# Attention and routed experts on one core: loads for eight heads at once, and traded halves in one block of keys

## The chip, the cores and the metric

One NeuronCore of a Trainium2 chip runs the whole program. The metric is the device time of one execution in microseconds. A kernel's time is the median of its runs; one more execution is taken by the profiler, and its times are the ones quoted from views of the profile.

## The reference

Attention over 8 batches with 8 heads, 576 positions and head size 64, where a position sees all keys of its own block of 64 and of the blocks before; then a mixture of 8 experts, in which each position is sent through one expert, chosen by its own logits or taken over from the position before it.

```python
scores = scale * np.matmul(q, k.transpose(0, 1, 3, 2))
mask = block_i >= block_j                      # pos // 64
scores = np.where(mask, scores, -1000000000.0)
attn = softmax(scores)
x = np.matmul(attn, v)                         # heads side by side: 512 columns
...
logits, local_gate = x @ w_gate, sigmoid(x @ w_local)
e = argmax(logits[b, s]) if s == 0 or local_gate[b, s] < 0.5 else prev_e
h = np.maximum(x[b, s] @ w1[e], 0.0)
out[b, s] = softmax(logits[b, s])[e] * (h @ w2[e])
```

The inputs and the result are float32; the expert weights are rounded to bf16 on the chip.

## The kernel before

**Tiles and loops.** The attention runs over 32 pairs of heads (pair `i` is batch `i // 4`, heads `2 * (i % 4)` and the next), in one loop in whose step `i` several stages lie side by side: the loads of `k` and `q` of pair `i + 2`, the value products of pair `i - 1`, the scores and exponentials of pair `i`, and the transposes of `k` and `q` of pair `i + 1`. Behind the attention come the experts, tile by tile of 128 positions. Routing steps on VectorE (DVE) are spread over the pairs.

**Scores and values.** Scores are held with keys on partitions and queries on columns. The 576 keys make chunks 0 to 3 of 128 keys and chunk 4 of 64. Within a chunk, `scores` computes each half of 64 keys apart, in float32 for two heads, so that four products of 64 x 64 stand in the four quarters of TensorE's array. The later half of a chunk is not seen by the chunk's first 64 queries. There chunk 0 holds the scores of chunk 4 instead, and the other chunks get a large negative number from a bf16 product (`minus` times `ones_b`, line 975), of which the exponential is zero. `values` then multiplies: for chunks 0 to 3 the list `VALUES` says from which query on and how many columns (two heads in the two column halves of the array, all 128 keys deep), and at the end, behind whatever is put `between`, come chunk 4 and the first 64 queries of chunk 0, 64 keys deep each, in the upper and the lower row half (line 1007). `add_chunks` sums the exponentials on VectorE for the denominators.

**Loads.** All loads of `q`, `k` and `v` are issued by SyncE (SP) in the program's order. `load_qk` brings the first 512 rows of `k` and `q` of a pair (256 KB each) into a staging place in the last two experts' part of `w2_bf`, and the 64 rows of the tail of each (32 KB) into a small tile `qkl`. GpSimd (POOL) rearranges the staged rows (`arrange`, line 880) before TensorE turns them (`transposes`, line 692, tiles `kq` and, for the tails, `o`). `load_v` brings `v` of a pair: two loads of 128 KB into a tile `v4`, with two buffers, and the 64 rows of the tail into `vl`. A load into a buffer waits until what was in it has been used; what stands behind it in SP's queue waits too.

**Weights.** The expert weights are loaded by POOL's queue (`load_weights`, lines 107 and 111), fourteen of the sixteen at every other pair from pair 2 on, each cast to 1 MB of bf16. The weights of experts 5 and 6 come at steps 22 to 28, so their places are empty until then. `w1_bf` and `w2_bf` have 4096 bf16 columns per expert (`WE`). In traces, all that lies in them is named `w_bf`: weights, staged `k` and `q`, routing scratch.

Of the kernel before, what the change touches and what calls it, by code (L numbers as in the profile page):

```python
# [62 lines left out]
def kernel(  # L63
# [41 lines left out]
    def load_weights(e, layer):  # L105
# [4 lines left out]
        else:  # L110
# [721 lines left out]
    with tc.tile_pool(name="atn_const", bufs=1) as cst, \  # L832
# [21 lines left out]

        raws, vs = ({} for _ in range(2))

        def load_qk(i):
            if i >= NPAIR:
                return
            b, p = divmod(i, HP)  # L860
            h2 = slice(2 * p, 2 * p + 2)
            tl = ld.tile([P, 2, D], F32, tag="qkl", name="qkl")
            raws[i] = [tl]
            for j, src in enumerate((k, q)):

                m = staged_of(i)[:, j].rearrange("p (h j d) -> p h j d", h=2, j=4)
                nc.sync.dma_start(
                    out=m.rearrange("p h j d -> p h (j d)"),
                    in_=src[b, h2, :512].rearrange("h (p j) d -> p h (j d)", j=4))
# [13 lines left out]
        def load_v(i):  # L883
            if i >= NPAIR:
                return
            b, p = divmod(i, HP)
            m = ld.tile([P, 4, 2, D], F32, tag="v4", name="v4", bufs=NV)
            for h in range(2):
                nc.sync.dma_start(
                    out=m[:, :, h, :],  # L890
                    in_=v[b, 2 * p + h, :512].rearrange("(so si) d -> si so d", si=P))
            nc.sync.dma_start(out=vls[i % NV][ST:],
                              in_=v[b, 2 * p:2 * p + 2, 512:].rearrange("h s d -> s h d"))
            vs[i] = [m[:, c] for c in range(4)] + [vls[i % NV]]
# [60 lines left out]
        def scores(i, u):  # L955
# [34 lines left out]
        def values(i, between=lambda: None):  # L990
# [2 lines left out]
            b, r = divmod(i + 1, HP)  # L993
            tail = (lambda: rows_of_batch(b - 2, (4,))) if r == 0 and 1 < b < B else lambda: lambda: None
            for c in range(NC - 1):
                for bk, q0, n in VALUES[c]:
                    for h in range(2):
                        nc.tensor.matmul(po[64 * h:64 * h + 64, VO + q0:VO + q0 + n],  # L998
                                         lhsT=vs[i][c][:, h, :],
                                         rhs=exps_at(i, c, q0, n, slice(0, P))[:, h, :],  # L1000
                                         start=(c == 0), stop=(c == 1 and not bk))
            out = tail()
            between()

            for c, rows, q0 in ((NC - 1, slice(ST, P), LAST), (0, slice(0, ST), 0)):
                for h in range(2):
                    nc.tensor.matmul(po[64 * h:64 * h + 64, VO + q0:VO + q0 + ST],  # L1007
                                     lhsT=vs[i][c][rows, h, :], rhs=Ss[i][rows, h, :ST],
                                     start=(c == 0), stop=True)
# [161 lines left out]
        def behind(i):  # L1171
# [114 lines left out]
    with ExitStack() as ffn:  # L1286
# [222 lines left out]
```

## Time and profile before

| | us |
|---|---|
| median of 3 runs | 414.41 (411.66, 414.41, 415.81) |
| profiled execution | 412.89 |
| its span, first to last instruction | 410.8 |
| its mean granted TensorE clock | 0.991 |
| attention | up to about 257 |
| experts | from there to the end |

Lines of a view read: engine, line of the kernel, operation, tile written <- tiles read, shapes, count, busy time, mean duration, idle time ahead. `PEld` is TensorE's loading of weights, which runs beside the products. A time in an order of time is the start, followed by the length of a merged group. `128*64` ahead of a shape is the part of the array: rows (keys or depth) times columns.

### The profile page before, as it was taken

To read this page: it belongs to the slowest core of one execution; us is meant where nothing else is said; L and a number is where in the kernel's file an instruction comes from. 1 tells how busy PE (TensorE), PEld (TensorE's weight loads), DVE (VectorE), ACT (ScalarE), POOL (GpSimd) and SP (SyncE) were. 2 spreads that over 40 slices of the span, in tenths; PEclk is the share of its full clock that TensorE was granted. 3 is DMA by queue.
4 is the path that set the end of the run, shared out by engine and by line. 5 is a ranking of instruction groups with operands and counts; after the bars stand their busy time and mean duration, and the time that the engine had idled before them with its cause. 6 is when DMAs were issued, how large, how long until landed. Compare 5 with 4: busy or idle time off the path is not lost. (4 is left out here: it accounts for less than half of the span.)

```text
span 410.8 us, 14546 instructions
## 1 busy us (share of the span) xinstructions
PE 395.0 (96%) x5834; PEld 285.7 (70%) x5834; DVE 246.2 (60%) x505; ACT 225.7 (55%) x391; POOL 183.8 (45%) x250
## 2 busy tenths in 40 slices
PE   8999999999999999999998998979999999999985
PEld 7677777776776876776774666647777777777663
DVE  3444746646646677977999767877985333324220
ACT  4666666665765765665663654334444455445342
POOL 1325343144144054554351452246767676666603
PEclk9999999999999999999998999999999999999989
DMA  6579999998998999999978789853753544554521
GB/s 180 135 155 225 195 214 245 206 187 227 215 207 192 207 184 222 208 167 239 205 153 199 131 162 192 124 136 111 159 173 104 152 148 131 142 158 138 140 67 77
DMA packets 108819, 69.97 MB, mean 170 GB/s; under 512 B 74847, under 2 KB 100255, under 8 KB 108752
## 3 DMA queue, kind: packets, MB, share of 16 engines
q0 software_dynamic: 19200, 34.84, 40.6%
q1 hardware_dynamic: 89552, 34.19, 35.9%
q8 instruction: 48, 0.79, 0.8%
q14 instruction: 19, 0.16, 0.1%
HBM read 66.88 MB, written 14.70 MB: 199 GB/s over the span
## 5 line engine op out<-in xcount | busy, mean ns | idle before, releaser
L1019 DVE TENSOR_TENSOR S<-S,Pc 128x896 f32<-128x896 f32 (+2 forms) x96 | 86.4, 900 | 21.4 <-PE o L998 16.5
L977 PE MATMUL sc<-qkT 64*64 64x224 f32 (+6 forms) x1536 | 92.1, 369 | 0.7 <-DVE xg L818 0.7
L1292 DVE COPY w1c<-w_bf 128x4096 bf16 x36 | 44.2, 1235 | 58.5 <-PE ps_y L1330 26.1
L1096 ACT ACTIVATE hT<-ps_h 128x512 bf16<-128x512 f32 x76 | 44.1, 598 | 57.6 <-PE ps_h L1093 23.1
L1093 PEld LDWEIGHTS <-w1c 128*128 128x128 bf16 x1152 | 67.9, 98 | 10.9 <-issue 3.8
L977 PEld LDWEIGHTS sc<-qkT 64*64 64x64 f32 x1536 | 70.6, 135 | 3.2 <-DVE xg L818 1.1
L880 POOL COPY w_bf<-w_bf 128x512 f32<-128x512 f32 x61 | 42.8, 718 | 66.5 <-DMA w_bf<-in_k_dram 27.4
L1330 PE MATMUL ps_y<-w_bf,hT 128*128 x296 | 71.3, 383 | 1.0 <-issue 0.7
L1093 PE MATMUL ps_h<-xT,w1c 128*128 128x128 bf16 x1088 | 67.2, 220 | 2.6 <-ACTq L1469 2.1
L651 POOL DMA_INDIRECT xg<-x_rows,idx x38 | 49.7, 1309 | 42.2 <-issue 13.9
L987 ACT ACTIVATE Pc<-sc 128x448 f32<-128x448 f32 (+1 forms) x96 | 68.1, 716 | 0.0
L998 PE MATMUL o<-Pc,v 128*64 128x320 f32 (+2 forms) x512 | 57.6, 366 | 0.0
L1338 POOL DMA_INDIRECT out_dram<-y,idx x37 | 42.4, 1147 | 25.7 <-issue 9.5
L998 PEld LDWEIGHTS o<-Pc,v 128*64 128x64 f32 x512 | 35.0, 137 | 23.8
L987 ACT ACTIVATE S<-sc 128x576 f32<-128x576 f32 x64 | 42.0, 656 | 14.9 <-PE sc L977 14.6
L1330 PEld LDWEIGHTS <-hT 128*128 128x128 bf16 x296 | 27.7, 99 | 28.5 <-issue 3.1
L1011 ACT COPY oT<-o 128x576 f32<-128x576 f32 x32 | 20.5, 641 | 36.2 <-PE o L1007 36.2
L1335 ACT ACTIVATE y<-ps_y,xg 128x512 f32<-128x512 f32 x37 | 25.4, 687 | 20.7 <-PE ps_y L1330 17.1
L818 DVE TENSOR_TENSOR xg<-trx,rs 128x512 bf16<-128x512 f32 (+1 forms) x31 | 20.2, 684 | 26.2 <-PE trx L692 26.1
L998 PE MATMUL o<-S,v 128*64 128x320 f32 (+1 forms) x256 | 35.0, 392 | 0.3 <-ACT qkT L925 0.3
L1026 POOL MEMSET S<- 64x128 f32 x30 | 6.0, 200 | 63.2 <-DVE S L1021 22.5
L946 ACT COPY qkT<-kq 128x1024 f32<-128x1024 f32 x30 | 30.8, 1027 | 0.4 <-PE trx L692 0.4
(313 smaller groups left out, 442.3 us busy)
## 6 DMA issues: line engine op xcount, KB each, us to landing
w_bf<-in_moe_w_dram POOLq DMA_DIRECT2D x16, 1024.0 KB
w_bf<-in_k_dram SPq DMA_DIRECT2D x32, 256.0 KB
w_bf<-in_q_dram SPq DMA_DIRECT2D x32, 256.0 KB
v<-in_v_dram SPq DMA_DIRECT2D x64, 128.0 KB
x_rows<-xg POOLq DMA_DIRECT2D x24, 128.0 KB
qkl<-in_k_dram SPq DMA_DIRECT2D x32, 32.0 KB
qkl<-in_q_dram SPq DMA_DIRECT2D x32, 32.0 KB
vl<-in_v_dram SPq DMA_DIRECT2D x32, 32.0 KB
```

The source lines that it names most:

```text
L651: st = nc.gpsimd.indirect_dma_start(out=x, out_offset=None, in_=x_dram[:rows], in_offset=bass.IndirectOffsetOnAxis(ap=row_of(ph, j), axis= ...
L880: copies[j](m, raws[i][1 + j].rearrange("p h j d -> p j h d"))
L946: nc.scalar.copy(to.rearrange("p a (r s) -> p r a s", r=2), ps.rearrange("p r (a s) -> p r a s", a=2))
L977: nc.tensor.matmul(to[:, col + skip:col + n], lhsT=t[r, 0, k0:k0 + ST], rhs=t[r, 1, q0 + skip:q0 + n], start=True, stop=True)
L987: nc.scalar.activation(exps_at(i, c, q0, n, rows), ps[rows, :, col:col + n], func=AF.Exp, scale=scale_attn)
L998: nc.tensor.matmul(po[64 * h:64 * h + 64, VO + q0:VO + q0 + n], lhsT=vs[i][c][:, h, :], rhs=exps_at(i, c, q0, n, slice(0, P))[:, h, :], st ...
L1019: nc.vector.tensor_add(Ss[i][:, :, P * c:], Ss[i][:, :, P * c:], Pc[i % 2][:, :, POS[c]:POS[c] + n])
L1093: nc.tensor.matmul(ps[:, fo, :], lhsT=w[:, ko * F + f0:ko * F + f0 + P], rhs=xT[:, ko, :], start=(ko == 0), stop=(ko == KO1 - 1))
L1096: relu[0] = nc.scalar.activation(hT[:, half * (FO // 2):(half + 1) * (FO // 2), :], ps, func=AF.Relu)
L1292: ended["w"] = nc.vector.tensor_copy(w, w1_bf[:, bass.ds(ev[i], WE)])
L1330: nc.tensor.matmul(ps, lhsT=hT[:, fo, :], rhs=w2_bf[:, bass.ds(ev + fo * Dm, Dm)], start=(fo == 0), stop=(fo == FO - 1))
L1338: st = nc.gpsimd.indirect_dma_start(out=out_flat, out_offset=bass.IndirectOffsetOnAxis(ap=row_of(ph, j), axis=0), in_=y, in_offset=None, b ...
```

## The change

For pairs 4 to 23 (batches 1 to 5, `WHOLE`), `v` and the tails of `k` and `q` are no longer loaded pair by pair. `load_whole`, called behind `load_v` in each of the four steps of a batch, brings one of four parts of the next batch, for eight heads at once: the tails of `k` and `q` (128 KB each), then `v` of chunks 0 and 1 (256 KB each), then chunk 2 (256 KB) and the later half of chunk 3 (128 KB), then the earlier half of chunk 3 and the tail (128 KB each). They lie in the places of expert 5 in `w1_bf` and `w2_bf`, by turns, and of expert 6 in `w1_bf`.

In these pairs chunk 3's keys trade partition halves: the later 64 keys are on partitions 0 to 63. `scores` computes the later half into the lower partitions, and `values` reads `VALUES_SW`: chunk 1 starts with 64 columns in place of 128, chunk 3 has 128 in place of 192. What is left out is added at the end, 64 keys deep: chunk 3's earlier keys for queries 384 to 447 in the upper row half, chunk 1's earlier keys for queries 128 to 191 in the lower one.

```diff
+    SW = 3
+    VALUES_SW = [VALUES[0],
+                 [(0, 128 + ST, ST), (1, QA, QB)],
+                 VALUES[2],
+                 [(1, 384 + ST, 128)]]
+    WHOLE = range(1, 6)
...
+        v_whole = [w[:, (E - 3) * WE:(E - 2) * WE].bitcast(F32).rearrange(
+            "p (c h d) -> p c h d", c=4, h=H) for w in (w1_bf, w2_bf)]
+        ends = w1_bf[:, (E - 2) * WE:(E - 1) * WE].bitcast(F32).rearrange(
+            "p (u h d) -> p u h d", u=4, h=H)
+        v_ends, qk_ends = ends[:, :2], ends[:, 2:]
+
+        def load_whole(b, part):
+
+            if b not in WHOLE:
+                return
+            rows = lambda x, r0, n: x[b, :, r0:r0 + n].rearrange("h s d -> s h d")
+            whole, high = v_whole[b % 2], slice(ST, P)
+            for out, x, r0, n in (
+                    ((qk_ends[:ST, b % 2], k, LAST, ST), (qk_ends[high, b % 2], q, LAST, ST)),
+                    ((whole[:, 0], v, 0, P), (whole[:, 1], v, P, P)),
+                    ((whole[:, 2], v, 2 * P, P), (whole[:ST, SW], v, SW * P + ST, ST)),
+                    ((whole[high, SW], v, SW * P, ST), (v_ends[high, b % 2], v, LAST, ST)))[part]:
+                nc.sync.dma_start(out=out, in_=rows(x, r0, n))
+
+        def swapped(i):
+            return i // HP in WHOLE
...
-            for j, src in enumerate((k, q)):
-                nc.sync.dma_start(out=tl[64 * j:64 * j + 64],
+            for j, src in enumerate((k, q) if not swapped(i) else ()):
+                nc.sync.dma_start(out=raws[i][0][64 * j:64 * j + 64],
...
+            if swapped(i):
+                h2 = slice(2 * p, 2 * p + 2)
+                vs[i] = [v_whole[b % 2][:, c, h2] for c in range(4)] + [v_ends[:, b % 2, h2]]
+                return
...
-                    late = half
+                    late = half ^ (c == SW and swapped(i))
...
-                for bk, q0, n in VALUES[c]:
+                for bk, q0, n in (VALUES_SW if swapped(i) else VALUES)[c]:
...
-            for c, rows, q0 in ((NC - 1, slice(ST, P), LAST), (0, slice(0, ST), 0)):
+            low, high = slice(0, ST), slice(ST, P)
+            of_s = ((NC - 1, high, LAST, Ss[i][high, :, :ST]), (0, low, 0, Ss[i][low, :, :ST]))
+            if swapped(i):
+                of_s = ((SW, high, SW * P, exps_at(i, SW, SW * P, ST, high)),
+                        (1, low, P, exps_at(i, 1, P, ST, low))) + of_s
+            for c, rows, q0, x in of_s:
...
             load_v(i + 1)
+            load_whole(i // HP + 1, i % HP)
```

On TensorE, the value products of pair 10, before. `S` and `Pc` hold exponentials, `v` and `vl` the values; the last two rows are the group of half depth. The rows give the output's partitions and columns, and how many products.

```order
L998 MATMUL o<-S,v_1209 64x192 x2
L998 MATMUL o<-S,v_1209 64x320 x2
L998 MATMUL o<-Pc_117,v_1209 64x128 x2
L998 MATMUL o<-Pc_117,v_1209 64x320 x4
L998 MATMUL o<-Pc_117,v_1209 64x192 x2
L705 MATMUL trg<-oT,wg_71 32x320 x4
L705 MATMUL trg<-S,sel 32x320 x8
L1007 MATMUL o<-S,vl_119 64x64 x2
L1007 MATMUL o<-S,v_1209 64x64 x2
```

The same place with the change, where the lines have moved (998 to 1032, 1007 to 1047) and the values lie in `w_bf`:

```order
L1032 MATMUL o<-S,w_bf 64x192 x2
L1032 MATMUL o<-S,w_bf 64x320 x2
L1032 MATMUL o<-Pc_117,w_bf 64x64 x2
L1032 MATMUL o<-Pc_117,w_bf 64x320 x4
L1032 MATMUL o<-Pc_117,w_bf 64x128 x2
L711 MATMUL trg<-oT,wg_71 32x320 x4
L711 MATMUL trg<-S,sel 32x320 x8
L1047 MATMUL o<-Pc_117,w_bf 64x64 x4
L1047 MATMUL o<-S,w_bf 64x64 x4
```

Two products lose half of their 128 columns, two lose 64 of 192, and the group at the end has eight products instead of four.

On SP, the loads from the small router weights `wg` on, before: `k` and `q` of pair 3 with their tails, `v` of pair 2, `k` and `q` of pair 4, and `v` of pair 3 without its tail.

```order
L1221 DMA wg_71<-in_moe_w_local_dram 64x4x1
L867 DMA w_bf<-in_k_dram 128x2x256
L867 DMA w_bf<-in_q_dram 128x2x256
L872 DMA qkl<-in_k_dram 64x2x64
L872 DMA qkl<-in_q_dram 64x2x64
L889 DMA v_325<-in_v_dram 128x4x64 x2
L892 DMA vl_119<-in_v_dram 64x2x64
L867 DMA w_bf<-in_k_dram 128x2x256
L867 DMA w_bf<-in_q_dram 128x2x256
L872 DMA qkl<-in_k_dram 64x2x64
L872 DMA qkl<-in_q_dram 64x2x64
L889 DMA v_384<-in_v_dram 128x4x64 x2
```

With the change, from `v` of pair 2 on (ahead of it, ahead of `wg`, two loads of 64x8x64 for the tails of batch 1 have come in):

```order
L923 DMA v_327<-in_v_dram 128x4x64 x2
L926 DMA vl_119<-in_v_dram 64x2x64
L880 DMA w_bf<-in_v_dram 128x8x64 x2
L897 DMA w_bf<-in_k_dram 128x2x256
L897 DMA w_bf<-in_q_dram 128x2x256
L923 DMA v_385<-in_v_dram 128x4x64 x2
L926 DMA vl_120<-in_v_dram 64x2x64
L880 DMA w_bf<-in_v_dram 128x8x64
L880 DMA w_bf<-in_v_dram 64x8x64
L897 DMA w_bf<-in_k_dram 128x2x256
L897 DMA w_bf<-in_q_dram 128x2x256
L880 DMA w_bf<-in_v_dram 64x8x64 x2
```

Between the `v` of pair 2 and the `k` of pair 4 now stand chunks 0 and 1 of batch 1's `v`, and ahead of pair 5's `k` chunk 2 and half of chunk 3; pair 4's and pair 5's own tails are gone.

More of the change, by code (lines that the diff above doesn't have):

```diff
@@ L1000, in values @@
                                          rhs=exps_at(i, c, q0, n, slice(0, P))[:, h, :],
-                                         start=(c == 0), stop=(c == 1 and not bk))
+                                         start=(c == 0),
+                                         stop=(c == 1 and not bk and not swapped(i)))
             out = tail()
             between()
-            for c, rows, q0 in ((NC - 1, slice(ST, P), LAST), (0, slice(0, ST), 0)):
+            low, high = slice(0, ST), slice(ST, P)
+            of_s = ((NC - 1, high, LAST, Ss[i][high, :, :ST]), (0, low, 0, Ss[i][low, :, :ST]))
+            if swapped(i):
+                of_s = ((SW, high, SW * P, exps_at(i, SW, SW * P, ST, high)),
+                        (1, low, P, exps_at(i, 1, P, ST, low))) + of_s
+            for c, rows, q0, x in of_s:
                 for h in range(2):
                     nc.tensor.matmul(po[64 * h:64 * h + 64, VO + q0:VO + q0 + ST],
-                                     lhsT=vs[i][c][rows, h, :], rhs=Ss[i][rows, h, :ST],
-                                     start=(c == 0), stop=True)
+                                     lhsT=vs[i][c][rows, h, :], rhs=x[:, h, :],
+                                     start=(c == 0), stop=c != SW)
             oTs[i] = op.tile([P, S], F32, tag="oT", name="oT", bufs=HP + 3)
```

5 lines of the change are left out of this document (3 added, 2 removed).

## The prediction

> **What bounds the kernel now.** I read the page first, then the busy time by stretch, then TensorE's groups of instructions by form, and last the order of time around the places that the diff touches.
>
> ```profile
> span 410.8 us, 14546 instructions
> PE 395.0 (96%) x5834; PEld 285.7 (70%) x5834; DVE 246.2 (60%) x505; ACT 225.7 (55%) x391; POOL 183.8 (45%) x250
> 60.00:100.00 40.00, 40.00 (x710) 29.74 (x703) 21.73 (x34) 26.62 (x48) 12.22 (x24) 1.00 1.02 222
> 100.00:150.00 50.00, 49.95 (x860) 35.84 (x860) 31.61 (x57) 30.64 (x55) 18.97 (x33) 1.00 0.96 197
> ```
>
> The first two lines are the page's, the others stretches of the attention stage (PE busy is the second figure, then the other engines, the granted clock and the DMA share). From 60 to 150 us TensorE (PE) has 89.95 of 90 us: there the end of the kernel moves by what its stream loses or gains. The DMA engines are as full (1.02, 0.96), so the second question is whether any load becomes late. The page's chain of waits covers only the last 15 us and says nothing here.
>
> **TensorE: the part that is shortened.** The change acts on pairs 4 to 23, 20 of 32. In each, the value products lose 64 columns in chunk 1 (128 to 64) and 64 in chunk 3 (192 to 128), for both heads, and gain four products of half depth and 64 columns. Groups of the stretch 34 to 190 us by form, with busy time and mean ns of one:
>
> ```profile
> L998 PE MATMUL o<-Pc,v 128*64 128x320 f32 x160 | 25.2, 432 | 0.0
> L998 PE MATMUL o<-Pc,v 128*64 128x192 f32 x84 | 10.7, 326 | 0.0
> L977 PE MATMUL sc<-qkT 64*64 64x192 f32 x80 | 9.8, 323 | 0.0
> L977 PE MATMUL sc<-qkT 64*64 64x128 f32 x80 | 9.2, 284 | 0.0
> L998 PE MATMUL o<-Pc,v 128*64 128x128 f32 x80 | 8.1, 273 | 0.0
> ```
>
> 432, 326 and 273 ns for 320, 192 and 128 columns: 0.83 ns a column. Each product is two instructions (80 for 20 pairs of two heads), so a product has two passes, and the order of time shows that the two heads share the time:
>
> ```profile
> 161.57 1.79 PE L998 MATMUL o<-Pc,v 128*64 128x128 f32 x16
> 163.29 0.48 PE L705 MATMUL trg<-oT,wg 128*32 128x320 f32 x4
> 171.70 0.27 PE L1007 MATMUL o<-S,vl 64*64 64x64 f32 x2
> 171.71 0.27 PE L1007 MATMUL o<-S,v 64*64 64x64 f32 x2
> 171.80 0.23 PE L1007 MATMUL o<-S,vl 64*64 64x64 f32 x2
> 171.82 0.23 PE L1007 MATMUL o<-S,v 64*64 64x64 f32 x2
> 171.88 0.27 PE L972 MATMUL sc<-qkT 64*64 64x64 f32 x2
> 171.94 0.27 PE L972 MATMUL sc<-qkT 64*64 64x64 f32 x2
> ...
> 174.06 0.19 PE L975 MATMUL sc<-ones_b,minus 64*64 64x64 bf16 x1
> 174.09 0.30 PE L977 MATMUL sc<-qkT 64*64 64x128 f32 x1
> ```
>
> From 161.57 to 163.29, 1.72 us, go 128 + 320 + 320 + 192 = 960 columns in two passes: 0.90 ns a column for both heads together. So 64 columns over two passes are 0.106 us by the first rate and 0.115 by the second. Chunk 3 saves 0.11. Chunk 1's rest is a pass of 64 columns, for which no full-depth row exists; the nearest is the quarter-array pass, 0.06 us from 171.88 to 171.94, so chunk 1 saves 0.11 - 0.06 a pass, 0.10 in two.
>
> The added products go into a group that is there already (line 1007), so the switch to half depth is paid once as before. That group has four products in two passes: starts at 171.70, 171.80, and the next work at 171.88. Its first pass takes 0.10, the second 0.08, and the pass between the two L972 rows 0.06. The group doubles: two passes more, 0.12 at the cheapest rate, 0.16 at the middle, 0.20 at the dearest. I take 0.12, since the added passes have neighbours of their own kind, as in the L972 rows. Values: 0.11 + 0.10 - 0.12 = 0.09 us a pair, bounds 0.01 and 0.11.
>
> [...]
>
> **TensorE: the score products of chunk 3.** Their number and columns stay, but the halves trade: the half with the bf16 mask block (64 columns of scores fewer) is now the lower one. Over unit 2 the lower half has 320 + 192 = 512 columns and the upper 256 + 128 with two mask blocks; afterwards both have 448. The unit ends with its longer half, so it may lose 64 columns less the mask block. The groups give 2 x (323 - 284) = 0.08 us for the two passes; the mask block holds up the pass behind it by 0.03 (174.06 to 174.09). I take 0.05, bounds 0 and 0.08.
>
> Sum on TensorE: 0.14 us x 20 = **2.8 us less**, bounds 0.2 (0.01 x 20) and 3.8 (0.19 x 20). ScalarE's exponentials and VectorE's sums keep their sizes.
>
> **The loads.** Bytes are the same over the whole kernel. Issues on SP's queue fall from 28 to 16 a batch, and four waits of a `v` load for its buffer a batch go; both are off the path and I cost them at nothing. What is new is the time at which bytes are asked for: during batch 0, whose own loads stay, batch 1 is loaded too. Ahead of pair 4's `k` stand 256 KB of tails and 512 KB of `v`; ahead of pair 5's another 384 KB. SP and GpSimd (POOL) there, and TensorE's use:
>
> ```profile
> 12.18 0.61 SPq L892 DMA_DIRECT2D vl<-in_v_dram  x1
> 12.88 0.60 SPq L1218 DMA_DIRECT2D wg<-in_moe_w_gate_dram  x1
> 20.83 0.55 SPq L867 DMA_DIRECT2D w_bf<-in_k_dram  x1
> 24.48 1.87 SPq L892 DMA_DIRECT2D vl<-in_v_dram  x1
> 26.45 0.54 SPq L867 DMA_DIRECT2D w_bf<-in_k_dram  x1
> 29.30 2.08 SPq L889 DMA_DIRECT2D v<-in_v_dram  x2
> ```
> ```profile
> 23.92 1.23 POOL L880 COPY w_bf<-w_bf 128x512 f32<-128x512 f32 x2 [1.77 <-DMA w_bf<-in_k_dram]
> 25.09 0.97 POOL L107 DMA_DIRECT2D w_bf<-in_moe_w_dram  x1
> 34.67 0.61 POOL L880 COPY w_bf<-w_bf 128x512 f32<-128x512 f32 x1 [8.61 <-DMA w_bf<-in_k_dram]
> 35.64 0.62 POOL L880 COPY w_bf<-w_bf 128x512 f32<-128x512 f32 x1 [0.36 <-DMA w_bf<-in_q_dram]
> 30.88 0.67 PE L692 MATMUL kq<-id_f,w_bf 64*128 64x64 f32 x16
> 37.18 0.67 PE L692 MATMUL kq<-id_f,w_bf 64*128 64x64 f32 x16
> ```
>
> Read from the bottom. TensorE turns pair 5's `k` and `q` at 37.18; POOL's two copies for it ended at 36.26. That is 0.9 us of margin, the smallest I found. Pair 5's `k` was issued at 26.45 and waited for: POOL's first load of expert weights, issued at 25.09 once pair 4's copies were through, took the engines. In the seven microseconds from 26 us (queue 0 the weights, queue 1 all of SP's loads: packets, MB, share of the engines):
>
> ```profile
> q0 software_dynamic: 490, 1.00, 83.6%
> q1 hardware_dynamic: 311, 0.14, 9.9%
> ```
>
> So `k` came 34.67 - 25.09 = 9.6 us after the weights' issue. Now the chain with the change. SP's whole queue moves its bytes at this rate (packets, MB, share of the engines over 410.8 us; below it a stretch):
>
> ```profile
> q1 hardware_dynamic: 89552, 34.19, 35.9%
> 8.00:24.00 16.00, 15.47 (x262) 11.01 (x260) 7.40 (x13) 10.90 (x20) 4.13 (x7) 1.00 0.59 153
> ```
>
> 34.19 MB in 0.359 x 410.8 = 147.5 us, 0.23 MB/us. 768 KB are 3.3 us, less pair 4's two tails of 32 KB, which are no longer loaded singly (0.3): pair 4's `k` and its copies come 3.0 us later, and with them the weights' issue: 28.1. Pair 4 itself isn't late: its copies ended at 25.15, and TensorE asks for them at 30.88. Pair 5's `k` then comes at 28.1 + 9.6 = 37.7, plus what part of the 384 KB still stands ahead of it when the weights are done, 0 to 1.6 us, say 0.8: 38.5. The copies end 1.6 us later (34.67 to 36.26), at 40.1. TensorE needs `k` copied at 37.18 and `q` half of its 0.6 us later, 37.5: **a wait of about 2.6 us** (40.1 less 37.5), bounds 0 and 4. Zero, because the engines are only 0.59 busy from 8 to 24 us: 6.6 us of room for the 3.0. Against zero: SP spends about 0.65 us on every issue there (12.18 to 12.88), one behind the other, so that the room is SP's own pace.
>
> After batch 1 the same bytes go in fewer issues and are asked for sooner, since no load of `v` waits for the value products before it; I see no second late load.
>
> [...]
>
> **Sum.** -2.8 + 2.6 = -0.2 us against the profiled execution's 412.89: 412.7. That execution lies 1.5 us under the median of the runs shown, 414.41 (411.66 to 415.81), and the mean of the four is 413.7; for the median of new runs I add 0.8: **413.5**.
>
> **Rivals.**
> [...]
> - *Slower: the wait halves the clock.* The trace has a place where TensorE idled for 1.86 of 3.45 us, and the next 3.42 us ran at half clock:
>
> ```profile
> 218.90:222.35 3.45, 1.59 (x31) 1.11 (x31) 3.38 (x8) 1.21 (x3) 1.08 (x2) 1.00 1.13 305
> 222.35:225.77 3.42, 3.41 (x36) 1.97 (x36) 3.15 (x6) 1.57 (x4) 0.00 (x0) 0.50 0.30 70
> ```
>
> That costs 3.42 x 0.5 = 1.7 us. [...] Then -2.8 + 2.6 + 1.7 = +1.5, own sum 414.4; with the wait at 4, +2.9, 415.8.
> - *The short products gain nothing* (each added pass costs 0.10, the mask block eats the scores): -0.2, and with the wait +2.4, own sum 415.3. The rows of 0.06 and of equal starts speak against it.
> - *The traded halves don't act on the scores*, since both halves are issued in one stream: -1.8 (0.09 x 20) instead of -2.8, with the wait +0.8.
>
> **How the numbers follow.** Within 1% (4.1 us of 414.41) is about what a measurement of this kernel can tell from no change. Chances: my forecast 0.40, no wait 0.25, half clock 0.20, no gain on TensorE 0.08, scores alone failing 0.07. No case passes 1% by itself; the spread of the runs (2.75 under the median, 1.4 over it) must help. No wait, at -2.8, needs 1.3 more: half of its chance, 0.12, and 0.08 from the rest, for gains that I haven't seen: faster 0.20. Half clock at +1.5 to +2.9, and the wait with no gain at +2.4, need 1.2 to 2.6 more: a third of 0.28, and 0.06 for late loads that I haven't found: slower 0.15. Same 0.65. The range goes from the no-wait case with a low run (410.1, rounded down to 409.8) to the half clock with the long wait and the median's distance (415.8 + 1.2): 409.8 to 417.0.
>
> **What would show it.** Pair by pair, values and the 64-column group must be 0.09 us shorter and the scores 0.05; half-depth passes at 0.06. At 37 us TensorE should wait for POOL's copies of pair 5, themselves waiting for `k`, with the weights' issue about 3 us later than 25.09. I am wrong if the passes cost 0.1, if there is no wait there, or if the clock halves at 38 to 45 us.

## The result and the profile after

| | before | after |
|---|---|---|
| median of new runs, 22 of each (us) | 412.44 | 416.79 |
| lowest to highest (us) | 408.84 to 421.45 | 412.90 to 424.22 |
| after / before | | 1.0102, 95% interval 1.0072 to 1.0132 |
| the same kernel again, later, on two chips | | 1.0050 (1.0012 to 1.0088); 1.0077 (1.0029 to 1.0124) |

The change makes the kernel slower, by 0.5 to 1.0%, 2 to 4 us. The forecast was 413.5, within 1% of before. The profiled run of the changed kernel took 424.22 us, 1.8% above its median, so its places are shown, and its sums are taken only together with a second profile (the run "again", 412.30 us).

The page after: span, busy time, then the DMA queues (packets, MB, share of 16 engines).

```profile
span 421.3 us, 14732 instructions
PE 392.5 (93%) x5972; PEld 287.2 (68%) x5994; DVE 243.1 (58%) x505; ACT 226.5 (54%) x391; POOL 185.6 (44%) x250
q1 hardware_dynamic: 88592, 34.19, 37.8%
```

TensorE (PE) is busy 2.5 us less than before (395.0), and the span is 10.5 us longer: the time went into waits (22 of the 5994 products left no record, so the busy time is a little low). The first wait is where the prediction put it. GpSimd (POOL) there, in order of time, with the idle time before an operation and what ended it:

```profile
27.28 0.61 POOL L910 COPY w_bf<-w_bf 128x512 f32<-128x512 f32 x1 [4.32 <-DMA w_bf<-in_k_dram]
28.14 0.63 POOL L910 COPY w_bf<-w_bf 128x512 f32<-128x512 f32 x1 [0.25 <-DMA w_bf<-in_q_dram]
28.72 0.97 POOL L107 DMA_DIRECT2D w_bf<-in_moe_w_dram  x1
38.13 0.61 POOL L910 COPY w_bf<-w_bf 128x512 f32<-128x512 f32 x1 [8.45 <-DMA w_bf<-in_k_dram]
41.66 0.62 POOL L910 COPY w_bf<-w_bf 128x512 f32<-128x512 f32 x1 [2.92 <-DMA w_bf<-in_q_dram]
```

SP's issues of pair 5's `k` and `q` in the same profile:

```profile
29.29 0.57 SPq L897 DMA_DIRECT2D w_bf<-in_k_dram  x1
29.96 0.41 SPq L897 DMA_DIRECT2D w_bf<-in_q_dram  x1
```

TensorE, its waits from 36 to 43 us (total, times, longest), and two stretches in the columns of the prediction's:

```profile
PE kq L698 <- POOL w_bf L910: 4.4, 2, 3.1
37.00:41.15 4.15, 0.93 (x19) 0.48 (x12) 0.00 (x0) 1.84 (x4) 0.61 (x1) 1.00 1.17 232
41.15:47.97 6.82, 5.64 (x36) 3.10 (x40) 2.49 (x7) 1.01 (x1) 5.54 (x19) 0.50 0.99 217
```

The weights were issued at 28.72, ahead of `k` (29.29) and `q` (29.96). `k` could be copied at 38.13 and `q` at 41.66, TensorE waited for both, 4.4 us, and 6.82 us from 41.15 on ran at half clock, which can cost up to 3.4 us more. Together they cost 7.4 us: from the first value products to pair 6's it takes 47.46 us here and 40.08 in again. The 6.82 us are twice the 3.42 at half clock in before (222.35 to 225.77). Here, as in before, the stretch ahead was not quite idle: 0.93 us of work in 4.15 here, 1.59 in 3.45 there.

The two queues in the same profile from 32 to 38 us, the weights' first, then SP's (packets, MB, share of the engines):

```profile
q0 software_dynamic: 442, 0.89, 81.0%
q1 hardware_dynamic: 445, 0.44, 27.0%
```

Each moved about as many packets as the other, but one of the weights holds 2 KB and one of SP's 1 KB. So SP's queue kept moving under the weights, at 0.07 MB/us, where the prediction has 0.23 for it alone. It was not always so: in before, from 28 to 30 us, the weights' queue moved 177 packets and SP's 3, although `k` had been issued at 26.45.

The products are what the prediction said of them. One pair (pair 11's values, then pair 12's; pairs count from 0) in before and in again, in order of time, one row for the start of each part:

```profile
92.23 1.08 PE L998 MATMUL o<-S,v 128*64 128x192 f32 x8
94.86 0.41 PE L692 MATMUL trx<-id_f,oT 64*64 64x64 f32 x8
95.21 0.27 PE L1007 MATMUL o<-S,vl 64*64 64x64 f32 x2
95.39 0.27 PE L972 MATMUL sc<-qkT 64*64 64x64 f32 x2
98.15 0.28 PE L692 MATMUL o<-id_f,qkl 64*128 64x64 f32 x2
98.87 0.38 PE L998 MATMUL o<-S,v 128*64 128x192 f32 x2
```
```profile
93.08 1.08 PE L1032 MATMUL o<-S,w_bf 128*64 128x192 f32 x8
95.51 0.41 PE L698 MATMUL trx<-id_f,oT 64*64 64x64 f32 x8
95.85 0.34 PE L1047 MATMUL o<-Pc,w_bf 64*64 64x64 f32 x8
96.15 0.27 PE L1006 MATMUL sc<-qkT 64*64 64x64 f32 x2
98.86 0.28 PE L698 MATMUL o<-id_f,w_bf 64*128 64x64 f32 x2
99.64 0.38 PE L1032 MATMUL o<-S,w_bf 128*64 128x192 f32 x2
```

From row to row: the full-depth values take 2.43 instead of 2.63, the half-depth group 0.30 instead of 0.18, the scores 2.71 instead of 2.76, and the stretch from the tails to the next values 0.78 instead of 0.72. So the values gain about 0.09 and the scores 0.05, as forecast, but the scores' part is given back ahead of the next values. ScalarE (ACT) shows why, before and then again:

```profile
98.10 0.56 ACT L987 ACTIVATE Pc<-sc 128x448 f32<-128x448 f32 x1
98.55 0.28 ACT L925 COPY qkT<-o 128x128 f32<-128x128 f32 x1
```
```profile
98.86 0.56 ACT L1021 ACTIVATE Pc<-sc 128x448 f32<-128x448 f32 x1
99.29 0.30 ACT L959 COPY qkT<-o 128x128 f32<-128x128 f32 x1
```

The values follow the end of the tails' copy by 0.05 us in both (98.83 to 98.87, 99.59 to 99.64), and that copy follows unit 1's exponentials, which lie ahead of chunk 3's scores and start 2.71 us behind the first scores in both. A pair is 0.09 us shorter, not 0.14: from pair 6's values to pair 18's, 12 pairs, before takes 91.14 us and again 90.02.

The last place lies behind the attention stage, where the prediction had nothing. POOL's last load of expert weights and TensorE's first product with them, before and then again:

```profile
248.79 0.93 POOL L111 DMA_DIRECT2D w_bf<-in_moe_w_dram  x1
262.54 1.89 PE L1330 MATMUL ps_y<-w_bf,hT 128*128 x8 [0.31 <-DMA w_bf<-in_moe_w_dram]
```
```profile
245.97 0.93 POOL L111 DMA_DIRECT2D w_bf<-in_moe_w_dram  x1
262.81 3.54 PE L1371 MATMUL ps_y<-w_bf,hT 128*128 x8 [3.08 <-DMA w_bf<-in_moe_w_dram]
```

The attention stage of again reaches this load 2.8 us earlier, and the product comes 0.3 us later. The same megabyte takes 3 us longer to land, with TensorE waiting.

### The profile page after: what moved, and what is told of

Same layout as the page of the kernel before. It is cut to its first block, busy times and chain, and to the rows that moved or that the text cites. A ratio compares the mean times of both kernels' runs of the same rounds, so it can differ in the third digit from the quotient of the medians.

```text
span 421.3 us, 14732 instructions
## 1 busy us (share of the span) xinstructions
PE 392.5 (93%) x5972; PEld 287.2 (68%) x5994; DVE 243.1 (58%) x505; ACT 226.5 (54%) x391; POOL 185.6 (44%) x250
## 4 chain that ended last, share of the span: by engine, by line
PE 78%; DMA 9%; DVE 5%; issue 3%; SPq 2%; POOL 1%; ACT 0%; POOLq 0%; DVEq 0%
PE o L1032 16%; PE sc L1011 16%; PE ps_h L1133 15%; PE ps_y L1371 14%; PE trg L711 5%; DMA w_bf<-in_moe_w_dram 4%; DMA w_bf<-in_q_dram 3%; PE kq L698 3%; PE o L1047 2%; PE trx L698 2%; DMA xT<-xg 2%; PE o L698 1%; PE sc L1006 1%; DVE xg L824 1%; SPq L880 1%
## 5 line engine op out<-in xcount | busy, mean ns | idle before, releaser
L1059 DVE TENSOR_TENSOR S<-S,Pc 128x896 f32<-128x896 f32 (+2 forms) x96 | 83.8, 873 | 22.5 <-PE o L1032 17.6
L1011 PE MATMUL sc<-qkT 64*64 64x224 f32 (+6 forms) x1536 | 89.8, 364 | 0.7 <-DVE xg L824 0.7
L1133 PEld LDWEIGHTS <-w1c 128*128 128x128 bf16 x1152 | 67.4, 98 | 13.2 <-issue 6.4
L1011 PEld LDWEIGHTS sc<-qkT 64*64 64x64 f32 x1536 | 72.2, 133 | 3.9 <-DVE xg L824 1.1
L657 POOL DMA_INDIRECT xg<-x_rows,idx x38 | 51.2, 1348 | 48.1 <-issue 19.0
L1371 PE MATMUL ps_y<-w_bf,hT 128*128 x274 | 65.8, 379 | 4.1 <-DMA w_bf<-in_moe_w_dram 2.8
L1021 ACT ACTIVATE S<-sc 128x576 f32<-128x576 f32 x64 | 42.0, 656 | 12.9 <-PE sc L1011 12.7
L1032 PE MATMUL o<-Pc,w_bf 128*64 128x320 f32 (+2 forms) x320 | 34.0, 351 | 1.3 <-issue 1.3
L1032 PEld LDWEIGHTS o<-Pc,w_bf 128*64 128x64 f32 x320 | 20.4, 142 | 17.7 <-issue 2.8
L720 ACT COPY LT<-trg 128x320 f32<-128x320 f32 x15 | 6.4, 426 | 46.0 <-PE trg L711 45.2
```

What stands on the lines that cost most here:

```text
L657: st = nc.gpsimd.indirect_dma_start(out=x, out_offset=None, in_=x_dram[:rows], in_offset=bass.IndirectOffsetOnAxis(ap=row_of(ph, j), axis= ...
L1011: nc.tensor.matmul(to[:, col + skip:col + n], lhsT=t[r, 0, k0:k0 + ST], rhs=t[r, 1, q0 + skip:q0 + n], start=True, stop=True)
L1021: nc.scalar.activation(exps_at(i, c, q0, n, rows), ps[rows, :, col:col + n], func=AF.Exp, scale=scale_attn)
L1059: nc.vector.tensor_add(Ss[i][:, :, P * c:], Ss[i][:, :, P * c:], Pc[i % 2][:, :, POS[c]:POS[c] + n])
L1133: nc.tensor.matmul(ps[:, fo, :], lhsT=w[:, ko * F + f0:ko * F + f0 + P], rhs=xT[:, ko, :], start=(ko == 0), stop=(ko == KO1 - 1))
L1371: nc.tensor.matmul(ps, lhsT=hT[:, fo, :], rhs=w2_bf[:, bass.ds(ev + fo * Dm, Dm)], start=(fo == 0), stop=(fo == FO - 1))
```

## The experiments

Each run was timed in five rounds, beside runs of before on its own chip (before2 has a profile only).

### First: the loads and the products apart

**again** is the changed kernel unchanged.

> The changed kernel once more, for a second profile. My theory: the cost lies in the attention stage, at fixed places: a wait of about 5 us for pair 5's k and q at 37 to 42 us, one half-clock stretch behind it (3.4 us of TensorE lost over two windows), and late v at about 114 to 122 us (2.5 us). Then all three stand in this profile too, the last value products of the attention stage end 4 to 6 us later than before's, and the stage behind it is as long as before's. Rival: the first profile's late places were that run's own; then they are elsewhere or smaller here, and part of the cost lies behind the attention stage. Ratio to before either way 1.007 to 1.013.

Measured: ratio 1.0050 (1.0012 to 1.0088). Its profile has no wait for pair 5, no half clock and no late `v`: the rival was right on those, the places were the first run's own. Weights were issued at 29.79 here, and pair 5's `k` at 29.57, ahead of them; it was copied at 33.92. TensorE also began later: the first value products start at 14.55 us, at 12.89 in the first profile, as its products ran slower at the very start (the four idle products ahead of the first scores took 1.22 us and not 0.71). What stayed is the wait for the last weights, 3.1 us (2.8 in the first profile).

**whole2** changes one line: `WHOLE = range(2, 6)`.

> Batches 2 to 5 only are loaded whole and trade halves; batch 1 is as before. My theory: it is the first batch's loads, asked for while batch 0's own still run, that cost; without them there is no wait for pair 5 and no half clock at 41 us, 16 pairs gain 0.14 us each (2.2 us), and at most the late v of the third batch (2.5 us) is left: ratio to before 0.994 to 1.001. Rival: every whole batch costs about the same (the change's 4.4 us and the 2.8 us gained, 7.2 in five batches); then four batches cost 5.8 less 2.2, and the ratio is about 1.008.

Measured: 1.0018 (0.9970 to 1.0065). No wait at pair 5, as expected, but the wait moved one batch on: 3.0 us for `v` in the values of pair 8, and a stretch of half clock with it, 4.7 us together. By this one profile it belongs to whichever batch is first, in which the batch ahead still has its own loads. The last weights were waited for 0.7 us.

**loads_only** keeps the loads; chunk 3's rows land in their old halves, and the products are before's:

```diff
-                    late = half ^ (c == SW and swapped(i))
+                    late = half ^ (c == SW and i // HP in TRADE)
-                for bk, q0, n in (VALUES_SW if swapped(i) else VALUES)[c]:
+                for bk, q0, n in (VALUES_SW if i // HP in TRADE else VALUES)[c]:
...
+    TRADE = ()
```

> The loads of the changed kernel, with the products of before: chunk 3's key blocks don't trade halves, and values and scores have their old sizes. My theory: the loads' cost and TensorE's gain add up, so this is the changed kernel plus 2.8 us: ratio to before about 1.017. Rival: TensorE waits for the loads at the end of its stretches anyway, and what it gains goes into the waits; then the ratio is the changed kernel's, 1.010.

Measured: 1.0001 (0.9953 to 1.0049). Neither: the change comes out no slower without its gain on TensorE than with it (the intervals overlap). In its profile pair 5's `k` came in time, and the values of pair 4 waited for the last part of `v`:

```profile
43.29 0.55 PE L1033 MATMUL o<-Pc,w_bf 128*64 128x192 f32 x4 [3.02 <-DMA w_bf<-in_v_dram]
```

From pair 6's values to pair 18's it takes 91.15 us (before 91.14): the loads cost nothing in the attention stage once the first batch is through, and half clock came behind this wait too (44.6 to 48.0 us). That the traded products gained nothing is what the third group follows.

**trade_only** keeps the products and loads pair by pair; chunk 3 comes in two issues of its own:

```diff
+            if b in TRADE:
+                for r0, s0 in ((ST, 0), (0, ST)):
+                    nc.sync.dma_start(out=m[r0:r0 + ST, SW],
+                                      in_=v[b, 2 * p:2 * p + 2, SW * P + s0:SW * P + s0 + ST].rearrange("h s d -> s h d"))
```

> The products of the changed kernel in batches 1 to 5, with the loads of before pair by pair; only chunk 3 of v is loaded in two parts with its halves traded (two more issues a pair on SP's queue, the same bytes). My theory: TensorE gains 0.14 us in 20 pairs, 2.8 us, and no load becomes late: ratio to before 0.993 (0.991 to 0.996). Rival: forty more issues of about 0.6 us each on SP's queue push k and q back, and the gain goes into waits: 0.998 to 1.01.

Measured: 1.0562 (1.0508 to 1.0617), the rival's direction and over five times its size. A pair has nine issues on SP's queue here and had seven; the tails, last among `k` and `q`, come late (TensorE's wait: total, times, longest), and seven stretches run at half clock (the mean granted clock of its profile is 0.972):

```profile
PE o L699 <- DMA qkl<-in_k_dram: 10.0, 5, 2.5
```

Loaded pair by pair in this way, the traded halves cost far more than they gain.

### Second: the weights one pair later

**odd_w** and its control **odd_before** issue every load of expert weights but the last of the fourteen one pair later:

```diff
-            if wload < 2 * E - 2 and i == 2 + 2 * wload:
+            if wload < 2 * E - 2 and i == min(3 + 2 * wload, NPAIR - 4):
```

> The changed kernel, with each load of expert weights issued one pair later (at pairs 3, 5, ... 27, and the last of these at 28 as before). My theory: what costs is the first burst of weights meeting batch 1's whole loads; whether pair 5's k or part 3 of v stands before or behind it in the queues decides between no wait and 4 to 7 us. Here the burst is issued behind the copies of pair 5, so both are ahead of it: no wait before 60 us, no half clock there, ratio to before 0.992 to 0.998. Rival: the late loads come from the doubled bytes of batch 0 alone, whatever the weights do, or move to the next place: a wait of 3 us or more between 30 and 60 us is still there, ratio 1.003 to 1.010.

> The kernel before, with the loads of expert weights issued one pair later in the same way: the control for the run above. My theory: there are no doubled loads here, so nothing changes, ratio 0.998 to 1.002. Rival: the later weights are worth something by themselves (0.995 or less), or they are missed at the end of the attention stage (1.004 or more).

Measured: odd_w 1.0107 (1.0061 to 1.0153), odd_before 1.0086 (1.0048 to 1.0124). The early wait is gone in odd_w, as my theory has it: from pair to pair it gains 0.09 us steadily up to pair 22. But the ratio is no better, and the control is slow by itself: from pair 22 to 23 TensorE waits for a mask on POOL (3.1 us in odd_before, 1.6 in odd_w), and in odd_before TensorE is slow behind this wait, as at half clock: eight products of line 705 take 0.74 us ahead of it, twelve take 2.35 behind it. The schedule was not a clean test. And odd_w waits 3.1 us for the last weights, odd_before not at all.

**again2** is the changed kernel, **before2** the one before.

> The changed kernel a third time, on this chip and in these rounds, for its median and a third profile. My theory: a race in batch 0 decides each run: when the weights' issue on POOL (about 29 us) comes ahead of SP's issue of pair 5's k, there is a wait of 3 to 5 us and a half clock at 37 to 48 us, otherwise none or one of 3 us for v; the median lies between, ratio 1.003 to 1.010. Rival: the early wait was peculiar to the first profile, and the cost is the wait for the last expert weights behind the attention stage (2.8 and 3.1 us in the two profiles, 0.3 in before's): then that wait is 2 to 3 us here too, with no early wait.

> The kernel before once more, for a second profile of it. My theory: no wait for pair 5, and the two half-clock stretches at 222 and 393 us are chance and stand elsewhere or not at all. Open: whether the wait for the last expert weights is 0.3 us again, or 2 to 3 us as in the two profiles of the changed kernel; in the second case that wait tells nothing of the change.

Measured: again2 1.0077 (1.0029 to 1.0124), with late `v` of 2.1 us in the first batch, 1.0 us at pair 14, and 2.2 us for the last weights; so both theories hold a part. before2 has no wait for the last weights. Its half clock stands at 223 us, where the first profile of before has it at 222; in no profile of the changed kernel does it stand there, and pairs 27 to 28 are 2.3 us shorter for it (11.14 in before, 8.84 in after). This gain nobody planned: TensorE idles there in both (1.9 us from 218.90 to 222.35 in before, 1.4 from 223 to 231 in after). Why the clock halves in one and not in the other was not tried.

### Third: where the code lies

The last weights came late in every profile with the traded products in five batches, and in none of before; in loads_only, without them, TensorE waited 2.1 us. What the late kernels but loads_only share is the number of instructions on TensorE. The page's row for the queue that loads code (packets, MB, share), before, then whole2, then after:

```profile
q8 instruction: 48, 0.79, 0.8%
```
```profile
q8 instruction: 49, 0.80, 0.8%
```
```profile
q8 instruction: 50, 0.82, 0.8%
```

0.79 MB in 48 packets are about 16 KB each. Before's 5834 matmuls and as many weight loads come to 243 of these instructions a packet; whole2 has 128 matmuls more, each with its weight load, 256 instructions, and one packet more. From these counts I take 128 matmuls with their weight loads as a block of code that comes in one packet; this is an estimate. The count alone does not follow so simply, though: pad_before and pad2_before below, with 64 instructions more, show 50 packets. After has 160 matmuls more, by the estimate a block and a quarter: from pair 24 on its blocks then begin elsewhere.

**trade4** trades in batches 2 to 5 (whole loads in 1 to 5), **trade4b** in 1 to 4: loads_only with another `TRADE`, and the rows of `v` to match. Both have 128 matmuls more.

> Whole loads in batches 1 to 5 as in the changed kernel, but the halves of chunk 3 trade in batches 2 to 5 only: 32 matmul instructions fewer on TensorE. So far the last load of expert weights (w2 of the last expert) took 12.4 to 13.1 us from its issue to its last packet in three profiles of kernels with the instruction count of before or of the run whole2, and 16.1 to 16.6 us in the four with the changed kernel's count; whole 16 KB blocks of code are fetched over the same DMA engines, and TensorE's count differs by a whole block between before and whole2, by a quarter block more in the changed kernel. My theory: it is the place of the code fetches and of the stalls beside them. Then this kernel takes about 13 us there, TensorE waits 1 us or less for it, and the ratio to before is 0.998 to 1.004 (the early late loads stay, 0 to 7 us). Rival: five batches of whole loads slow the end themselves: 16 us, a wait of 2 to 3 us, ratio 1.006 to 1.012.

> As trade4, but the halves trade in batches 1 to 4 instead of 2 to 5: the same count of instructions. My theory (place of the code): the last weights' load takes about 13 us as in trade4, ratio 0.998 to 1.006. Rival: the traded products of batch 1 are what slows the end, or trade4's 13 us was chance: 15 us or more.

**pad_before**, **pad2_before** and **pad_after** change idle products at the start alone (the diff is pad2_before's):

```diff
-        idle_products(7)
+        idle_products(4, 19)
...
+            for j in range(short):
+                nc.tensor.matmul(ps[:16, 0, :16], lhsT=zeros[:, :16], rhs=zeros[:, :16], start=True, stop=True)
```

(pad_before has `ps[:, 0, :1]`, `lhsT=zeros`, `rhs=zeros[:, :1]`; pad_after `idle_products(1, 54)`.)

> The kernel before, with 32 matmul instructions more at its start (19 products of one column for 3 of the idle products), where TensorE waits for its first load: TensorE's code is shifted by a quarter block as in the changed kernel, and nothing else is changed. My theory (place of the code): the last weights' load takes 16 us instead of 12.4 to 13.1, TensorE waits 2 to 3 us for it, ratio 1.004 to 1.010. Rival: the slow end belongs to the change's own loads or products: 12.4 to 13.1 us, no such wait, ratio 0.999 to 1.003.

> The kernel before, shifted once more by 32 matmul instructions, now with small weights (16 columns) so that the start moves by about 1 us and not by 8.2. My theory (place of the code on TensorE): the last weights' load takes 14.4 to 16.6 us from issue to last packet, TensorE waits 1.5 to 3 us for it; ratio 1.003 to 1.010. Rival: it takes 12.4 to 13.1 us as in three profiles of before and its control, and what pad_before showed (14.4) came from its late start.

> The changed kernel with 96 matmul instructions more at its start (54 small products for 6 of the idle ones), which with the change's own makes two whole blocks of code against before. My theory: the last weights' load takes 12.4 to 14 us instead of 16.1 to 16.6, and TensorE waits 1 us or less; the start moves by up to 4 us, and pair 5 is then not late. From the first value products to the end it is 2 to 3 us shorter than the run again. Rival: 16 us as in all four profiles with the changed products in five batches.

Measured, with the last weights' time from issue to last packet and TensorE's wait for them in the profile, by the shift of TensorE's code in matmuls against before; 128 is a block, by the estimate above:

| run | shift | landing (us) | wait (us) | ratio |
|---|---|---|---|---|
| before, before2, odd_before | 0 | 13.1, 12.4, 12.6 | 0.3, 0, 0 | |
| loads_only | 0 | 14.6 | 2.1 | 1.0001 |
| whole2, trade4, trade4b | 128 | 13.1, 13.0, 12.9 | 0.7, 0, 0 | 1.0018, 1.0026, 1.0071 |
| after, again, again2, odd_w | 160 | 16.3, 16.2, 16.6, 16.4 | 2.8, 3.1, 2.2, 3.1 | |
| trade_only | 160 | 15.8 | 2.3 | |
| pad_before | 32 | 14.4 | 1.6 | 1.0236 |
| pad2_before | 32 | 16.3 | 3.2 | 1.0093 (1.0041 to 1.0145) |
| pad_after | 256 | 13.2 | 0.5 | 0.9980 (0.9940 to 1.0020) |

pad2_before, and then pad_after, the same two rows as above:

```profile
249.51 0.94 POOL L111 DMA_DIRECT2D w_bf<-in_moe_w_dram  x1
266.51 3.32 PE L1332 MATMUL ps_y<-w_bf,hT 128*128 x8 [3.21 <-DMA w_bf<-in_moe_w_dram]
```
```profile
246.94 0.93 POOL L111 DMA_DIRECT2D w_bf<-in_moe_w_dram  x1
260.97 1.89 PE L1373 MATMUL ps_y<-w_bf,hT 128*128 x8 [0.54 <-DMA w_bf<-in_moe_w_dram]
```

Thirty-two small matmuls more at the start, which compute nothing, make before's last weights land as late as the changed kernel's; ninety-six more in the changed kernel bring them back, and the stage behind attention to 152.1 us. The traces fit: in all seven profiles with a shift of 32 or 160, two of the 16 KB code packets start between the issue of the last weights and their landing, 1.2 to 3.9 and 9.5 to 12.4 us after the issue. With a whole number of blocks it is one, 5.0 to 9.5 us after it (before has a second, 0.1 us ahead of the last packet).

Two things keep this short of a proof. loads_only, at shift 0, landed after 14.6 us. And the pads move more than the code: TensorE's first value products start 1.7 us later than before's in pad2_before and 1.3 later than after's in pad_after. Against the start as the cause of the landing speak pairs of profiles of the same shift whose starts differ by 1.6 us: after and again landed after 16.3 and 16.2 us, trade4b and trade4 after 12.9 and 13.0. For pad_after's ratio of 0.998 it cannot be set aside: its profile has no late load in the first batch either, like the others that start late.

trade4b's 1.0071 has another cause in its profile: the wait for pair 5 (3.9 us), which trade4's, with its first values at 14.50 and not 12.95, has not. pad_before's ratio is mostly its start: 38 products of one column took 8.11 us, so that its values began 8.2 us late.

### Fourth: a version from both causes

**cand_a4** (trade4) moves the weights one pair later up to pair 19, with two pairs in a row at 19 and 20. **cand_b** (whole2) does so from pair 6 on and leaves the first two loads at pairs 2 and 4. The line of cand_a4, then of cand_b:

```diff
+            if wload < 2 * E - 2 and i == (*range(3, 20, 2), 20, 22, 24, 26, 28)[wload]:
...
+            if wload < 2 * E - 2 and i == (2, 4, *range(7, 20, 2), 20, 22, 24, 26, 28)[wload]:
```

> The run whole2 (batches 2 to 5) with the loads of expert weights one pair later from pair 6 to pair 19, two pairs in a row at 19 and 20, and as before from 22 on. My theory: the burst no longer meets the doubled loads of batch 1, so the wait for v at pair 8 (3.0 us) and its half clock (1.7 us) go, 16 pairs gain 0.14 us, and the end is as in whole2: ratio to before 0.990 to 0.996. Rival: the doubled burst at pairs 19 and 20, or masks on POOL behind the weights' issue (3.1 us in the run odd_before), take it back: 0.999 or more.

> The run trade4 with the loads of expert weights one pair later up to pair 19, two pairs in a row at 19 and 20, and as before from 22 on. My theory: no wait for pair 5 and none for v of batch 1, 16 pairs gain 0.14 us, and the end is as in whole2: ratio to before 0.990 to 0.996. Rival: as for cand_b, or the slow end of the changed kernel comes with five batches of whole loads: 1.000 or more.

Measured: 0.9985 (0.9945 to 1.0025) and 0.9974 (0.9937 to 1.0012), between theory and rival. In both profiles no load is late in the first whole batch. But cand_a4's profile, 416.56 us where its median is 410.25, loses 3.7 us at pairs 17 to 19, with a wait of 2.1 us at 146 us for which it shows no releaser; the rival's double burst is issued at 157 and 165 us, behind it. Their last weights took 15.2 and 15.7 us at a shift of a whole block, more than I expected.

**cand_c4** (trade4) and **cand_c** (pad_after) move the first two loads only: `i == (3, 5, *range(6, 29, 2))[wload]`.

> The run trade4 with the first two loads of expert weights one pair later (pairs 3 and 5 instead of 2 and 4), all others as before. My theory: what is left of the cost in trade4 and trade4b (1.003 and 1.007; one profile with a wait of 4 us for pair 5, one without) is the race of the first burst of weights with batch 1's whole loads. Here no run has it: the profile shows no wait for pair 5 or for v of batch 1, the last weights take 12.4 to 14 us, and the ratio to before is 0.990 to 0.996. Rival: the two bursts at pairs 5 and 6 make the next loads late in its place, ratio 0.998 or more.

> The run pad_after (traded halves in batches 1 to 5, code shifted by 96 more matmul instructions at the start) with the first two loads of expert weights one pair later. My theory: no late load, 20 pairs gain 0.14 us, the last weights take about 13 us, and the pads cost about 1.5 us at the start: 0.990 to 0.997. Rival: pad_after had no late load anyway, since its start is 1.5 us later, and nothing is gained over its 0.998.

Measured: cand_c4 **0.9924 (0.9889 to 0.9959)**, 405.59 us beside 409.59 for before; cand_c 0.9933 (0.9898 to 0.9968). Both beat before, and by their ratios the changed kernel. POOL in cand_c4:

```profile
33.41 0.92 POOL L911 COPY w_bf<-w_bf 128x512 f32<-128x512 f32 x1 [3.15 <-DMA w_bf<-in_k_dram]
34.93 0.61 POOL L911 COPY w_bf<-w_bf 128x512 f32<-128x512 f32 x1 [0.59 <-DMA w_bf<-in_q_dram]
35.74 0.98 POOL L107 DMA_DIRECT2D w_bf<-in_moe_w_dram  x1
```

Pair 5's copies are through before the first burst is issued, and neither of the two profiles has a wait for it. cand_c's last weights took 12.9 us, without a wait; cand_c4's 15.3, with 2.8, although its code lies a whole block off: this part of my expectation failed.

What the gain is made of is open. Beside before's profile, from another chip, cand_c4's is 5.0 us shorter: 0.3 from the first values to pair 24's, 3.1 from there to pair 31's, where before has its half clock at 222 us, and 1.7 behind, where before has another at 393; its start is 0.1 later. And the control is missing: no run has the kernel before with its first two weights' loads one pair later, so that the schedule may be worth something without the change.

## Why the prediction was wrong

The sum was -2.8 + 2.6, and both terms were mis-sized: TensorE gains 1.9 us, and the first batch's late loads, with the half clock behind them, are not a constant 2.6 but anything from about 0 to 7.4. And two costs were put at nothing: a second late load, and the last weights behind the attention stage. That stage, whose end the prediction left as it was, is 2.1 to 5.0 us longer.

- **TensorE's values, -0.09 a pair:** right. Sixteen half-depth instructions take 0.30 us, 19 ns each, where before's eight take 0.18. The switch to half depth, which both kernels have once a pair, is about 0.1 us in before: two passes of 192 columns start at 171.27 and 171.43, the half-depth group at 171.70, 0.27 behind in place of 0.16.
- **TensorE's scores, -0.05 a pair:** right where it was measured, and given back before the next values, which wait for ScalarE. I took the bounds from TensorE's stream alone, since it had 89.95 us of work in 90. So 20 pairs gain 1.9 us and not 2.8.
- **The wait for pair 5:** the mechanism was right, with the weights' issue at 28.72 (forecast 28.1) and `k` copied from 38.13 (38.5 landed). The size was off: 4.4 us instead of 2.6, above the bound of 4. The step that failed put `q` half of 0.6 us behind `k`; it came 3.5 us behind (41.66 less 38.13). `k`, issued 0.57 us behind the weights, came 8.8 us after its issue. The prediction had the weights take the engines, with 83.6% beside 9.9% in before. In this trace, from 32 to 38 us, the two queues moved as many packets as each other, 442 beside 445, and the wait is there all the same, with the weights' packets twice as large; in before, from 28 to 30 us, it was 177 beside 3. And the wait is a race, not a constant. Seven profiles have whole loads and the weights' issue of pair 2 against them. In the two with the weights issued ahead of pair 5's `k` (after, trade4b) TensorE waits for pair 5, 4.4 and 3.9 us; in the five with `k` ahead it waits 0.4 us at most. Of these five, the two that start normally (first values at 12.8 us: again2, loads_only) wait 2.1 and 3.0 us for `v`, and the three whose TensorE starts later (14.2 to 14.6: again, trade4, pad_after) at most 0.2. In the four with the first weights moved behind 35 us (odd_w, cand_a4, cand_c4, cand_c) no load of the first batch is late. Over the three profiles of the changed kernel the loads up to pair 24 cost 9.4, about 0 and 6.0 us (how much later pair 24's values begin than in before, less the shift at the start, plus the 1.9 gained); the half clock and the loads about pair 14 are in these figures.
- **The half clock behind it**, a rival at 0.20 and 1.7 us: it came in the first profile, over 6.82 us, worth 3.0 us (7.4 less the wait of 4.4). How long a wait it takes is not shown: from 268.07 to 271.49 in the same profile TensorE idled for 2.79 of 3.42 us, and the granted clock was 1.00 there and in all that followed up to 420 us. The one at before's 222 us is missing with the change and gave 2.3 us back.
- **"After batch 1 ... I see no second late load":** wrong in two of three profiles: after and again2 take 2.3 and 2.7 us longer than again from pair 13's values to pair 15's. What makes them late was not tried.
- **What the sum did not have:** the last weights. The stage behind attention takes 153.1 and 152.9 us in the profiles of before and 155.2 to 158.1 in those of the changed kernel, which is the one cost that all three have in common. The wait for the last weights is 2.2 to 3.1 us of it; what else lengthens after's by 5.0 us was not followed. Padding moves the landing in both directions with the kernel's loads unchanged, and the runs without pads follow the shift as well, so the place of TensorE's code is very likely a cause. Not the only one: loads_only and three of the last four runs landed after 14.6 to 15.7 us with their code a whole number of blocks off. By what way the place acts (the packets of code themselves, or what they collide with) stays open.

Put together for again, from its profile against before's: the start +1.8, the products -1.9, the missing half clock -2.3, the rest of the attention stage -0.1, the stage behind it +2.1: about -0.4, where the two spans differ by 0.4. That is a run without a late load; the two profiles with late loads have 6 to 9 us on top.

## What to carry to other kernels

A wait that one profile shows at the start of a new way of loading may be a race: look at which of two issues came first, and move the one that can wait: with two weights' loads a pair later the ratios fall by 0.5% (pad_after to cand_c, whose intervals overlap) and 1.0% (trade4 to cand_c4), though on another chip, and with the control missing. Where a stage ends with a transfer that lands just in time, its margin is a term of the sum; read it before trusting any gain ahead of it. And before a change of 1% is put down to what it computes, shift the code by a few idle instructions in both kernels.

## What the runs showed of the hardware

- Thirty-two idle matmuls more at the start made before 0.9% slower (pad2_before, 1.0093). Not all of it can be the place of the code: in its profile the first values start 1.7 us later, and TensorE waits 3.2 us for the last weights where before waits 0.3.
- A product of one column with full weights costs about as much as one of 128: 38 took 8.11 us at the start of pad_before, 0.213 each, and the eight of 128 columns ahead of them 1.83, 0.229 each. In pad_after, 108 of 16 columns with weights of 16 columns took 3.06 us, 0.028 each.

```profile
0.80 2.04 PE L1114 MATMUL idle<-const-float32-0.0 128*128 128x128 f32 x8 [0.80 <-PEq L1495]
2.63 8.11 PE L1116 MATMUL idle<-const-float32-0.0 128*128 128x1 f32 x38
```
```profile
1.49 3.06 PE L1156 MATMUL idle<-const-float32-0.0 128*16 128x16 f32 x108
```
